# Strided attention and routed experts on one core: the values' products of two heads taken as one, with a block-diagonal second operand

## The chip, the cores and the metric

The kernel runs on one core of one Trainium2 chip. The metric is the device time of one execution in microseconds (us), measured on the chip. The engines are named as the profile names them: PE is TensorE's matmuls, PEld its weight loads, DVE is VectorE, ACT ScalarE, POOL GpSimd, SP SyncE, which here only issues transfers. All operands of the attention part are float32; a float32 matmul stands in the trace as two weight loads and two passes of the moving operand (the page counts each), a transpose as one of each.

## The reference

Attention over 8 batches, 8 heads, 576 positions, head dimension 64, and then a top-1 mixture of 8 experts on its rows. The first four heads see the last 32 positions, the other four see every 32nd position up to their own:

```
scores = scale * np.matmul(q, k.transpose(0, 1, 3, 2))
rel = pos[:, None] - pos[None, :]
mask_local = (rel >= 0) & (rel < stride)
mask_strided = (rel >= 0) & (pos[None, :] % stride == pos[:, None] % stride)
masks = np.stack([mask_local if h < H // 2 else mask_strided for h in range(H)], axis=0)
...
attn = np.matmul(attn / (sum + 1e-09), v)
x = attn.transpose(0, 2, 1, 3).reshape(B * S, H * D)
...
h = np.maximum(x[mask] @ w1[e], 0.0)
out[mask] = gate_w * eom * (h @ w2[e])
```

## The kernel before, in words

The attention part walks 40 steps, five for each batch (t = 5b + j). Rows of queries are cut into tiles: a strided tile has 64 rows (54 of them used: three residues of 18 rows) against 64 keys, a local tile 32 rows against 64 keys. Steps j = 0 and 1 hold only strided tiles, j = 3 and 4 only local tiles, j = 2 both. Each step holds two "windows" w of 128 rows, two pairs of heads i and in each pair two heads h. Head h = 0 of a pair lives on partitions 0 to 63 and head h = 1 on partitions 64 to 127, in queries (q_t), keys (kbs strided, kbl local) and values (vst strided, vlt and vev local: vlt as loaded, vev shifted by 32 positions by the copies of `even`).

A step is a chain over the engines that is worked off over five steps, so that PE always has several steps in hand. `scores` (L253) makes the products of queries and keys into sp, head by head: 64 rows of contraction, 64 or 32 rows of output. `bar` and `top` on DVE add the mask and take row maxima, `shift` on POOL subtracts them, `expo` on ACT takes the exponential. Two steps later `turn_p` transposes the probabilities on PE (four transposes of 128x128, in which the two heads of a pair come to lie on the two halves of the partitions) and `evac_p` copies them to SBUF as pt. Three steps later `values` (L304) multiplies pt with the values, and the column of ones behind each head's 64 values gives the sum of its row. Four steps later `norm` on DVE divides and writes x_t, `rows` sends x_t to DRAM (xd), `turn_x` transposes it and `evac_x` copies it, for the experts' logits (`logits`, L379) and the gating chain.

`values` takes each head by itself. Its loop is

```
for i, p0, m, n, h in packed(j, w):
    nc.tensor.matmul(out=xv[p0:p0 + m, h, w, i, :], lhsT=pt[half(h), w, i, p0:p0 + m],
                     rhs=value(b, i, h, m, n), start=True, stop=True)
```

where `half(h)` is the 64 partitions of a head: 64 rows of contraction, 64 (strided) or 32 (local) columns of weights, 65 moving columns. A strided step has 16 such matmuls, a local one 32, the mixed one 20. The two heads of a pair use the two row halves of the array, and the tiles at different p0 use different column groups. The outputs of head 0 and head 1 go to two banks of xp.

The order is written out by hand (`manual_schedule`): in each step PE runs scores of step t, turn_p of t - 2, values of t - 3, turn_x of t - 4, with pieces of the logits and the gating chain between them (`pump`). SP issues all loads of a batch: at j = 1 vst and at j = 3 vlt of the next batch (`load_v`, L209), one transfer over 128 partitions each; the two copies of vst and vlt alternate between batches. ACT issues no transfer in this part.

After the 40 steps a tail finishes the last batch, ranks the experts and starts the first expert's layer; then the experts' part (L751 to L791) runs matmuls over all 128 rows of the array to the end.

Of the kernel before, what the change touches and what calls it, by code (L numbers as in the profile page):

```python
# [7 lines left out]
F32 = mybir.dt.float32  # L8
# [9 lines left out]
B, H, S, D = 8, 8, 576, 64  # L18
# [12 lines left out]
NG = 11  # L31
# [26 lines left out]
def attn_moe_kernel(  # L58
# [109 lines left out]
    def attention():  # L168
        with ExitStack() as actx:
# [13 lines left out]
            kbl = [kv.tile([128, 2, 2, HS + 32], F32, name=f"kbl{i}") for i in range(2)]  # L183
            vlt = [kv.tile([128, NL, 2, D + 1], F32, name=f"vlt{i}") for i in range(2)]
            vst = [kv.tile([128, NG, 2, D + 1], F32, name=f"vst{i}") for i in range(2)]
            vev = kv.tile([128, NL, 2, D + 1], F32, name="vev")

            qts = {}

            def load_s(b, cs=slice(0, WS)):  # L190
# [18 lines left out]
            def load_v(b, ts, src):  # L209
                nc.sync.dma_start(out=ts[b % 2], in_=src[b])  # L210

            def even(b, eng, h, f):

                ps = slice(D * h + 32 * f, D * h + 32 * (f + 1))
                copy = nc.scalar.copy if eng is nc.scalar else eng.tensor_copy
                copy(out=vev[ps, f:NL].rearrange("p n i e -> p (n i e)"),
                     in_=vlt[b % 2][ps, 0:NL - f].rearrange("p n i e -> p (n i e)"))

# [10 lines left out]
            col0 = lambda g: 54 * g - 18 if g else 0  # L229

            half = lambda h: slice(D * h, D * (h + 1))

# [12 lines left out]

            def value(b, i, h, m, n):
                return (vst[b % 2] if m == 64 else vlt[b % 2] if n % 2 else vev)[half(h), n if m == 64 else n // 2, i, :]

# [55 lines left out]
            def values(b, j):  # L304
                pt = pt_.pop((b, j))
                xp = ps_x.tile([128, 2, 512], F32, name="xp")
                xv = xp[:, :, 0:260].rearrange("p h (w i e) -> p h w i e", w=2, i=2)
                for w in range(2):
                    for i, p0, m, n, h in packed(j, w):
                        nc.tensor.matmul(out=xv[p0:p0 + m, h, w, i, :], lhsT=pt[half(h), w, i, p0:p0 + m],  # L310
                                         rhs=value(b, i, h, m, n), start=True, stop=True)
                xp_[b, j] = xp[:, :, 0:260].rearrange("p h (g e) -> p h g e", g=4)

            def norm(b, j, part):
# [4 lines left out]
                if part == 0:  # L319
                    nc.vector.tensor_scalar(out=rs[:, 0], in0=xp[:, :, :, D], scalar1=1e-9, scalar2=None, op0=ALU.add)  # L320
                elif part == 1:
                    nc.vector.reciprocal(out=rs[:, 1], in_=rs[:, 0])
                else:
                    x_t = xp_p.tile([128, 2, 4, D], F32, name="x_t")
                    nc.vector.tensor_tensor(out=x_t.rearrange("p w (i h) d -> p h (w i) d", h=2), in0=xp[:, :, :, 0:D],
                                            in1=rs[:, 1].unsqueeze(3).to_broadcast([128, 2, 4, D]), op=ALU.mult)
                    x_[b, j] = x_t.rearrange("p w h d -> p w (h d)")
# [265 lines left out]
            nc.sync.dma_start(out=ident, in_=ident_in)  # L593
            for h in range(2):
                nc.vector.memset(vev[D * h + 32:D * (h + 1), 0], 0.0)
            load_v(0, vst, vs)
            load_v(0, vlt, vl)
            load_s(1)
            setup()

            ns = B * NS
            t = 0
            while t < ns:
# [29 lines left out]
                for h in ((0,) if b and j == 3 else (1,) if b and j == 4 else (0, 1) if t == 4 else ()):  # L633
                    even(b, nc.scalar, h, 1)
                    even(b, nc.vector, h, 0)
                at(expo, 0)
                if t + 1 < len(WARM):
                    warm(WARM[t + 1])
# [365 lines left out]
```

## Time and profile before

| | |
|---|---|
| time, three runs | 711.96, 713.33, 718.02 us; median 713.33 us |
| the profiled execution | 715.86 us; its span 714.2 us, so 1.66 us lie around the span |
| mean granted TensorE clock | 0.954 of full speed |
| busy in the span | PE 649.9 us (91%), PEld 541.1, DVE 306.0, ACT 260.8, POOL 187.3 |
| attention, 5 to 197 us | PE busy 149.3 us of 192 |
| experts, 260 us to the end | PE busy 446.5 us of 454 |

The busy time of PE counts passes whose ends are modelled and which overlap, so a PE that is busy all the time is not one at its peak: what counts is the distance between the starts of passes. "issue" as a releaser is time in which an engine stood still and waited for nothing that the profile shows. The granted clock of a stretch stands in the column PEclk of the table of stretches.

### The profile page before, as it was taken

The numbers are of one execution on the slowest core, as the hardware profiler recorded it, in microseconds if no ns is written. First come the engines' busy times: TensorE is split into PE (matmuls) and PEld (weight loads), VectorE is DVE, ScalarE is ACT, GpSimd is POOL, SyncE is SP. The second block draws the span as 40 slices with busy tenths as digits, with TensorE's granted clock in tenths as the row PEclk, the third lists the DMA queues.
The fourth block names the chain that finished last, engine by engine and source line by source line (L and its number), as shares of the span: only waits on it lengthen the run. The fifth ranks groups of instructions, "written<-read, shape, count | busy, mean of one in ns | idle before, by whom it ended". The sixth has DMA issues, their size and how long they took to land.

```text
span 714.2 us, 16814 instructions
## 1 busy us (share of the span) xinstructions
PE 649.9 (91%) x6965; PEld 541.1 (76%) x6965; DVE 306.0 (43%) x673; ACT 260.8 (37%) x483; POOL 187.3 (26%) x191
## 2 busy tenths in 40 slices
PE   6786877987777799999999999999999999999995
PEld 5564555655554588799879988988987987987984
DVE  3576657776544442433224232422633433432410
ACT  2464445445431431433323332423423423433420
POOL 3123354456342430140113013012201401301001
PEclk9799999897987899999999999999999999999998
DMA  8667556558524226352235133324524514521000
GB/s 313 258 213 251 156 194 225 168 170 271 160 67 146 56 73 216 118 182 60 90 104 154 40 134 121 117 58 144 153 75 133 160 31 140 163 96 58 15 14 38
DMA packets 42420, 95.26 MB, mean 133 GB/s; under 512 B 7219, under 2 KB 18067, under 8 KB 42344
## 3 DMA queue, kind: packets, MB, share of 16 engines
q1 hardware_dynamic: 33176, 71.24, 31.2%
q0 software_dynamic: 8048, 19.79, 8.5%
q10 hardware_dynamic: 1120, 3.15, 1.3%
q8 instruction: 55, 0.90, 0.5%
q14 instruction: 21, 0.17, 0.1%
HBM read 74.55 MB, written 20.47 MB: 133 GB/s over the span
## 4 chain that ended last, share of the span: by engine, by line
PE 61%; issue 23%; DMA 5%; POOL 4%; DVE 4%; SPq 1%; ACT 1%; another core or an unknown queue 1%; POOLq 0%; DVEq 0%; ACTq 0%
PE yp L774 22%; PE hp L758 20%; PE xp L310 4%; DMA xd<-x_t 4%; PE sp L258 4%; PE xtp L354 3%; PE tp L294 2%; PE sp L470 2%; POOL out_dram L791 2%; PE tp L748 2%; PE gp L386 1%; DMA kbl<-in_kl_dram 1%; POOL xg L153 1%; DVE p_t L270 1%; PE gp L395 1%
## 5 line engine op out<-in xcount | busy, mean ns | idle before, releaser
L758 PE MATMUL hp<-xh,w1l 128*128 128x256 f32 (+1 forms) x480 | 148.1, 309 | 0.0
L758 PE MATMUL hp<-xl,w1h 128*128 128x256 f32 (+1 forms) x480 | 148.0, 308 | 0.0
L758 PE MATMUL hp<-xh,w1h 128*128 128x256 f32 (+1 forms) x480 | 147.9, 308 | 0.0
L791 POOL DMA_INDIRECT out_dram<-ys,tab x40 | 41.9, 1047 | 352.1 <-ACT ys L790 340.9
L758 PEld LDWEIGHTS hp<-xh,w1h 128*128 128x128 f32 x480 | 91.2, 190 | 2.1
L758 PEld LDWEIGHTS hp<-xl,w1h 128*128 128x128 f32 x480 | 91.1, 190 | 1.9
L758 PEld LDWEIGHTS hp<-xh,w1l 128*128 128x128 f32 x480 | 91.0, 189 | 1.4
L774 PE MATMUL yp<-w2h,hhb 128*128 128x512 f32 (+3 forms) x208 | 83.9, 403 | 0.0
L774 PE MATMUL yp<-w2l,hhb 128*128 128x512 f32 (+3 forms) x208 | 82.2, 395 | 0.0
L774 PE MATMUL yp<-w2h,hlb 128*128 128x512 f32 (+3 forms) x208 | 81.7, 393 | 0.0
L696 DVE TENSOR_TENSOR xl<-tp,xh 128x512 fp32r<-128x512 f32 (+3 forms) x40 | 25.7, 650 | 114.4 <-ACT xh L695 114.4
L281 POOL TENSOR_TENSOR p_t<-p_t,st 128x512 f32<-128x512 f32 x40 | 47.2, 1179 | 104.0 <-DVE st L277 46.7
L762 DVE SCALAR_TENSOR_TENSOR hlb<-hp,hhb 128x480 fp32r<-128x480 f32 (+7 forms) x64 | 34.7, 541 | 84.9 <-ACT hhb L761 72.5
L761 ACT ACTIVATE hhb<-hp 128x480 fp32r<-128x480 f32 (+7 forms) x64 | 30.6, 478 | 100.7 <-PE hp L758 94.2
L695 ACT CAST xh<-tp 128x512 fp32r<-128x512 f32 (+3 forms) x40 | 21.8, 555 | 124.0 <-PE tp L748 124.0
L552 POOL DMA_INDIRECT table<-meta,dst x48 | 44.6, 929 | 30.7 <-DVE ew L497 13.3
L774 PE MATMUL yp<-w2h,hha 128*128 128x512 f32 x128 | 51.0, 398 | 0.0
L774 PE MATMUL yp<-w2h,hla 128*128 128x512 f32 x128 | 50.6, 395 | 0.0
L774 PE MATMUL yp<-w2l,hha 128*128 128x512 f32 x128 | 50.4, 394 | 0.0
L153 POOL DMA_INDIRECT xg<-xd,tab x40 | 44.8, 1119 | 17.8 <-issue 16.3
L287 ACT ACTIVATE p_t<-p_t 128x512 f32<-128x512 f32 x40 | 25.2, 630 | 61.1 <-POOL p_t L281 61.0
L762 DVE SCALAR_TENSOR_TENSOR hla<-hp,hha 128x256 fp32r<-128x256 f32 x56 | 23.6, 422 | 54.4 <-ACT hha L761 54.3
(134 smaller groups left out, 1068.5 us busy)
## 6 DMA issues: line engine op xcount, KB each, us to landing
raw<-in_moe_w_dram SPq DMA_DIRECT2D x54, 512.0 KB
vst<-in_vs_dram SPq DMA_DIRECT2D x8, 715.0 KB
kbl<-in_kl_dram SPq DMA_DIRECT2D x8, 640.0 KB
vlt<-in_vl_dram SPq DMA_DIRECT2D x8, 585.0 KB
q_t<-in_ql_dram SPq DMA_DIRECT2D x8, 576.0 KB
xd<-x_t SPq DMA_DIRECT2D x80, 54.0 KB
q_t<-in_qs_dram SPq DMA_DIRECT2D x7, 586.0 KB
kbs<-in_ks_dram SPq DMA_DIRECT2D x7, 586.0 KB
```

The lines of the kernel that those rows point to most:

```text
L153: nc.gpsimd.indirect_dma_start(out=dst, out_offset=None, in_=src, in_offset=bass.IndirectOffsetOnAxis(ap=idx, axis=0), bounds_check=top, o ...
L258: nc.tensor.matmul(out=sv[p0:p0 + m, h, w, i, :], lhsT=query(b, i, h, m, n), rhs=keys(b, i, h, m, n), start=True, stop=True)
L281: nc.gpsimd.tensor_tensor(out=p_[b, j], in0=p_[b, j], in1=sp_.pop((b, j)).unsqueeze(3).to_broadcast([128, 2, 4, 64]), op=ALU.subtract)
L287: nc.scalar.activation(out=p_t, in_=p_t, func=AF.Exp, scale=scale)
L310: nc.tensor.matmul(out=xv[p0:p0 + m, h, w, i, :], lhsT=pt[half(h), w, i, p0:p0 + m], rhs=value(b, i, h, m, n), start=True, stop=True)
L552: i = nc.gpsimd.indirect_dma_start(out=table[:, :], out_offset=bass.IndirectOffsetOnAxis(ap=dst[:, j:j + 1], axis=0), in_=meta[:, b * NB + ...
L696: nc.vector.tensor_tensor(out=lo, in0=src, in1=f32(hi), op=ALU.subtract)
L758: nc.tensor.matmul(out=hp[:, 0:n], lhsT=w[:, k, 128 * j:128 * (j + 1)], rhs=x[:, k, 0:n], start=first, stop=(k == KC - 1 and w is w1l))
L761: nc.scalar.activation(out=hh[:, j, 0:n], in_=hp[:, 0:n], func=AF.Relu)
L762: nc.vector.scalar_tensor_tensor(out=hl[:, j, 0:n], in0=hp[:, 0:n], scalar=0.0, in1=f32(hh[:, j, 0:n]), op0=ALU.max, op1=ALU.subtract)
L774: nc.tensor.matmul(out=yp[0:m, :], lhsT=h[:, j, o:o + m], rhs=w[:, j, :], start=(j == 0 and q == 0), stop=(j == FC - 1 and q == 2))
L791: i = nc.gpsimd.indirect_dma_start(out=out[:, :], out_offset=bass.IndirectOffsetOnAxis(ap=tab[:, 2:3], axis=0), in_=ys[0:m, :], in_offset= ...
```

## The change

The two heads of a pair are multiplied at once. The tiles of values get a new axis h in front (128, 2, n, 2, 65): partitions 0 to 63 hold head 0's values under h = 0 and zeros under h = 1, partitions 64 to 127 hold zeros under h = 0 and head 1's values under h = 1. One matmul then contracts over all 128 partitions of pt, and its 130 moving columns give both heads' 65 columns side by side. `scores` stays one head at a time. The layout of xp becomes one bank per window w instead of one per head, so `norm` writes x_t in plain order.

The zeros are written once per buffer by a new function `clear`: at the start for vlt[0] and vev on ACT (four copies of a zero column over 64 partitions x 1170 elements), for vst[0] on DVE and POOL (one memset each of 64 x 1430), and behind `expo` of steps 5 and 7 for vst[1] and vlt[1] on DVE and POOL. The loads write only the halves that hold values, so the zeros stay. `load_v` therefore needs two transfers in place of one: SP issues the half of head 0, ACT that of head 1, in the same places of the program. `even` copies the half of its head only.

```diff
-            vlt = [kv.tile([128, NL, 2, D + 1], F32, name=f"vlt{i}") for i in range(2)]
-            vst = [kv.tile([128, NG, 2, D + 1], F32, name=f"vst{i}") for i in range(2)]
-            vev = kv.tile([128, NL, 2, D + 1], F32, name="vev")
+            vlt = [kv.tile([128, 2, NL, 2, D + 1], F32, name=f"vlt{i}") for i in range(2)]
+            vst = [kv.tile([128, 2, NG, 2, D + 1], F32, name=f"vst{i}") for i in range(2)]
+            vev = kv.tile([128, 2, NL, 2, D + 1], F32, name="vev")
+
+            def clear(t, spare=False):
+                if spare:
+                    for ps, h in ((slice(0, D), 1), (slice(D, 128), 0)):
+                        o = t[ps, h].rearrange("p n i e -> p (n i e)")
+                        nc.scalar.copy(out=o, in_=zeros[ps, 0:1].to_broadcast([D, o.shape[1]]))
+                else:
+                    nc.vector.memset(t[0:D, 1], 0.0)
+                    nc.gpsimd.memset(t[D:128, 0], 0.0)
+                if t is vev:
+                    nc.vector.memset(t[32:D, 0, 0], 0.0)
+                    nc.gpsimd.memset(t[D + 32:128, 1, 0], 0.0)
...
             def load_v(b, ts, src):
-                nc.sync.dma_start(out=ts[b % 2], in_=src[b])
+                for h, eng in ((0, nc.sync), (1, nc.scalar)):
+                    eng.dma_start(out=ts[b % 2][half(h), h], in_=src[b, half(h)])
...
-            def value(b, i, h, m, n):
-                return (vst[b % 2] if m == 64 else vlt[b % 2] if n % 2 else vev)[half(h), n if m == 64 else n // 2, i, :]
+            def value(b, i, m, n):
+                return (vst[b % 2] if m == 64 else vlt[b % 2] if n % 2 else vev)[:, :, n if m == 64 else n // 2, i, :]
...
             def values(b, j):
                 pt = pt_.pop((b, j))
                 xp = ps_x.tile([128, 2, 512], F32, name="xp")
-                xv = xp[:, :, 0:260].rearrange("p h (w i e) -> p h w i e", w=2, i=2)
                 for w in range(2):
-                    for i, p0, m, n, h in packed(j, w):
-                        nc.tensor.matmul(out=xv[p0:p0 + m, h, w, i, :], lhsT=pt[half(h), w, i, p0:p0 + m],
-                                         rhs=value(b, i, h, m, n), start=True, stop=True)
-                xp_[b, j] = xp[:, :, 0:260].rearrange("p h (g e) -> p h g e", g=4)
+                    for i in range(2):
+                        for p0, m, n in tiles(j, w):
+                            nc.tensor.matmul(out=xp[p0:p0 + m, w, 130 * i:130 * (i + 1)],
+                                             lhsT=pt[:, w, i, p0:p0 + m], rhs=value(b, i, m, n), start=True, stop=True)
+                xp_[b, j] = xp[:, :, 0:260].rearrange("p w (h e) -> p w h e", h=4)
...
-                    nc.vector.tensor_tensor(out=x_t.rearrange("p w (i h) d -> p h (w i) d", h=2), in0=xp[:, :, :, 0:D],
+                    nc.vector.tensor_tensor(out=x_t, in0=xp[:, :, :, 0:D],
...
+            for v in (vlt[0], vev):
+                clear(v, spare=True)
+            clear(vst[0])
             load_v(0, vst, vs)
             load_v(0, vlt, vl)
...
+            clears = {5: vst[1], 7: vlt[1]}
...
                 at(expo, 0)
+                if t in clears:
+                    clear(clears[t])
```

What it does to the order of instructions, in three places. First PE, in steps 4 and 5, from the values of a strided step to the beginning of the values of the mixed one (xp is the product of values, xtp the transposed x_t, sp the scores, tp the transposed probabilities; behind each name the shape of output rows and moving columns). Before:

```order
L310 MATMUL xp<-vst_132,pt 64x65 x16
L354 MATMUL xtp<-ident,x_t 128x128 x4
L258 MATMUL sp<-kbs_127,q_t 64x64 x16
L294 MATMUL tp<-ident,p_t 128x128 x4
L310 MATMUL xp<-vst_132,pt 64x65 x8
L310 MATMUL xp<-vev,pt 32x65 x2
L310 MATMUL xp<-vlt_130,pt 32x65 x2
L310 MATMUL xp<-vst_132,pt 64x65 x2
```

and with the change:

```order
L322 MATMUL xp<-vst_132,pt 64x130 x8
L366 MATMUL xtp<-ident,x_t 128x128 x4
L270 MATMUL sp<-kbs_127,q_t 64x64 x16
L306 MATMUL tp<-ident,p_t 128x128 x4
L322 MATMUL xp<-vst_132,pt 64x130 x4
L322 MATMUL xp<-vev,pt 32x130
L322 MATMUL xp<-vlt_130,pt 32x130
L322 MATMUL xp<-vst_132,pt 64x130
```

Nothing changes its place; the products of values are half as many, with twice the columns, and everything else on PE is as it was.

Second ACT, in steps 7 and 8 of the program, around the load of vlt (xt takes the transposed x_t, pt the transposed probabilities, p_t is the exponential's tile). Before:

```order
L369 COPY xt<-xtp 128x6x18 x2
L372 COPY xt<-xtp 128x2x64
L373 COPY xt<-xtp 128x2x2x18
L301 COPY pt<-tp 128x512
L287 ACTIVATE p_t<-p_t 128x512
L363 COPY xt<-xtp 128x2x256
```

and with the change:

```order
L381 COPY xt<-xtp 128x6x18 x2
L384 COPY xt<-xtp 128x2x64
L385 COPY xt<-xtp 128x2x2x18
L313 COPY pt<-tp 128x512
L299 ACTIVATE p_t<-p_t 128x512
L224 DMA vlt_130<-in_vl_dram 64x1170
L375 COPY xt<-xtp 128x2x256
```

A transfer of 64 partitions now stands in ACT's queue between an exponential and the copy that frees xtp; the same happens at j = 1 with vst.

Third DVE, in steps 5 and 6, where a buffer of the second batch is cleared (rs holds the reciprocal row sums, st the maxima). Before:

```order
L270 TENSOR_TENSOR p_t<-sp,mask 128x2x4x64
L277 TENSOR_REDUCE st<-p_t 128x8
L320 TENSOR_SCALAR rs<-xp 128x8
L322 RECIPROCAL rs<-rs 128x8
L325 TENSOR_TENSOR x_t<-xp,rs 128x2x4x64
```

and with the change:

```order
L282 TENSOR_TENSOR p_t<-sp,mask 128x2x4x64
L289 TENSOR_REDUCE st<-p_t 128x8
L194 MEMSET vst_133 64x1430
L332 TENSOR_SCALAR rs<-xp 128x8
L334 RECIPROCAL rs<-rs 128x8
L337 TENSOR_TENSOR x_t<-xp,rs 128x512
```

A memset of 64 x 1430 has come in between the maxima of one step and the normalisation of the next, and x_t is written in one plain run.

More of the change, by code (lines that the diff above doesn't have):

```diff
@@ L183, in attention @@
             kbl = [kv.tile([128, 2, 2, HS + 32], F32, name=f"kbl{i}") for i in range(2)]
-            vlt = [kv.tile([128, NL, 2, D + 1], F32, name=f"vlt{i}") for i in range(2)]
-            vst = [kv.tile([128, NG, 2, D + 1], F32, name=f"vst{i}") for i in range(2)]
-            vev = kv.tile([128, NL, 2, D + 1], F32, name="vev")
+            vlt = [kv.tile([128, 2, NL, 2, D + 1], F32, name=f"vlt{i}") for i in range(2)]
[12 more added lines that the diff above has]
+                    nc.gpsimd.memset(t[D + 32:128, 1, 0], 0.0)
             qts = {}
+            half = lambda h: slice(D * h, D * (h + 1))
             def load_s(b, cs=slice(0, WS)):
@@ L215, in even @@
                 copy = nc.scalar.copy if eng is nc.scalar else eng.tensor_copy
-                copy(out=vev[ps, f:NL].rearrange("p n i e -> p (n i e)"),
-                     in_=vlt[b % 2][ps, 0:NL - f].rearrange("p n i e -> p (n i e)"))
+                copy(out=vev[ps, h, f:NL].rearrange("p n i e -> p (n i e)"),
+                     in_=vlt[b % 2][ps, h, 0:NL - f].rearrange("p n i e -> p (n i e)"))
             loc, srd = slice(0, 2), slice(2, 4)
@@ L229, in attention @@
             col0 = lambda g: 54 * g - 18 if g else 0
-            half = lambda h: slice(D * h, D * (h + 1))
             def query(b, i, h, m, n):
@@ L593, in attention @@
             nc.sync.dma_start(out=ident, in_=ident_in)
-            for h in range(2):
-                nc.vector.memset(vev[D * h + 32:D * (h + 1), 0], 0.0)
+            for v in (vlt[0], vev):
+                clear(v, spare=True)
+            clear(vst[0])
             load_v(0, vst, vs)
```

## The prediction

> **What bounds the kernel now.** I read the page's shares first, then the table of stretches, then who PE waited for, then the chain of waits in order of time.
>
> ```profile
> PE 649.9 (91%) x6965; PEld 541.1 (76%) x6965; DVE 306.0 (43%) x673; ACT 260.8 (37%) x483; POOL 187.3 (26%) x191
> q8 instruction: 55, 0.90, 0.5%
> ```
>
> Two numbers matter here. PE and PEld together execute 13930 instructions, and one queue carries 55 packets of 0.90/55 MB = 16 KB of instructions: one packet for 253 of PE's instructions. [...]
>
> ```profile
> 5.00:197.00 192.00, 149.28 (x4041) 110.00 (x4040) 125.17 (x336) 89.91 (x190) 78.22 (x74) 0.90 0.65 218
> 260.00:714.00 454.00, 446.45 (x2543) 391.38 (x2542) 150.14 (x237) 148.63 (x253) 84.53 (x85) 1.00 0.34 105
> ```
>
> The columns are the length, then busy time and count of PE, PEld, DVE, ACT and POOL, then granted clock, DMA share and GB/s. The experts' 454 us are bound by PE at full clock, and the change does not touch them. In the attention part PE is busy for 149 of 192 us and the clock is 0.90; no other engine is near its limit (DVE 125 of 192). So PE is the longest engine there, but 43 us of it are waits. The waits of PE in that stretch (us in total, times, longest):
>
> ```profile
> PE xp L310 <- issue: 14.6, 12, 4.3
> PE sp L258 <- issue: 8.7, 7, 2.4
> PE tp L294 <- issue: 4.2, 3, 2.7
> ...
> PE xtp L354 <- issue: 1.0, 1, 1.0
> ```
>
> 14.6 + 8.7 + 4.2 + 1.0 = 28.5 us in 23 waits are "issue": PE waits for no engine and no transfer of data. 4041 + 4040 instructions are 31.9 blocks of 253 in these 192 us, one per 6.0 us, 0.9 us of wait for each. I take these waits for the arrival of the next block of instructions. In the chain of waits (start, length, what) the long ones stand as
>
> ```profile
> 16.05 4.26 issue
> ...
> 25.04 1.70 issue
> ...
> 61.72 2.60 issue
> ...
> 69.67 1.96 issue
> ...
> 94.48 1.36 issue
> ```
>
> and behind each of these comes a stretch at half clock:
>
> ```profile
> 20.40:23.70 3.30, 3.30 (x104) 2.68 (x105) 2.66 (x6) 0.70 (x2) 0.05 (x1) 0.50 1.00 382
> 27.30:33.90 6.60, 6.60 (x116) 4.77 (x116) 3.58 (x7) 2.37 (x5) 1.04 (x1) 0.50 0.46 164
> ...
> 64.80:68.10 3.30, 3.30 (x85) 1.86 (x76) 0.85 (x3) 0.86 (x2) 1.24 (x2) 0.50 1.02 380
> 71.60:74.90 3.30, 3.27 (x41) 1.90 (x44) 1.06 (x3) 1.64 (x4) 1.84 (x2) 0.50 0.27 85
> 95.60:98.90 3.30, 3.06 (x41) 2.55 (x41) 0.35 (x1) 1.91 (x3) 2.83 (x3) 0.50 0.36 116
> 126.30:132.90 6.60, 6.60 (x140) 4.97 (x136) 4.20 (x17) 2.16 (x5) 3.14 (x4) 0.50 0.26 65
> 170.70:180.70 10.00, 9.42 (x182) 7.19 (x183) 4.29 (x11) 2.73 (x6) 4.68 (x5) 0.50 0.89 281
> ```
>
> PE is busy for 35.6 us in these seven stretches, so they cost about 17.8 us. The first five (19.5 us busy, 9.8 us lost) follow waits for instructions; the last two follow other waits. The attention part is thus PE's own work, plus waits for instructions, plus the slow clock that they leave behind.
>
> **The change part by part.** *The array's work.* What a pass costs is read from these rows of PE in order of time (start, length of the group, count), with the length of a single pass (min/median/max, ns) behind them:
>
> ```profile
> 42.33 0.69 PE L386 MATMUL gp<-xt,wgt 128*32 128x288 f32 x8
> 42.95 0.86 PE L258 MATMUL sp<-kbl,q_t 64*32 64x64 f32 x64
> ...
> 44.65 0.70 PE L310 MATMUL xp<-vst,pt 64*64 64x65 f32 x32
> ...
> 231.25 2.86 PE L470 MATMUL sp<-xe,raw 128*128 128x256 f32 x12 [0.78 <-DVE hla L477]
> ```
>
> ```profile
> L386 PE MATMUL gp<-xt,wgt x128: 403/430/690, 42.3 to 224.2; 128*32 128x288 f32 x128
> ```
>
> ```profile
> L310 PEld LDWEIGHTS xp<-vst,pt x704: 128/135/228, 15.4 to 203.8; 64*64 64x64 f32 x176
> L310 PE MATMUL xp<-vst,pt x704: 213/219/368, 15.4 to 203.9; 64*64 64x65 f32 x176
> ...
> L310 PE MATMUL xp<-vev,pt x576: 213/220/314, 28.8 to 217.2; 64*32 64x65 f32 x192
> ...
> L310 PE MATMUL xp<-vlt,pt x576: 213/237/314, 28.8 to 217.3; 64*32 64x65 f32 x192
> ```
>
> On the whole array 12 passes of 256 columns take 2.86 us; without the last one's 0.38 that is 11 distances of 0.225, or 0.88 ns per column. The eight passes of the logits (L386, all 128 rows, 32 columns of the array each) start within 0.69 - 0.43 = 0.26 us: two rounds of 288 columns x 0.88 = 0.25, so four tiles that lie side by side in the columns do run together. This row carries over to the new products, which also use all rows and 32 or 64 columns of the array.
>
> A round of 65 columns is 0.057 us, one of 130 is 0.114 us. Before, a strided step's 32 passes sit on 4 tiles of 64x64: 8 rounds, 0.46 us, and the row shows 0.70 - 0.22 = 0.48 us. Afterwards 16 passes sit on 2 tiles of 128x64: 8 rounds again, but of 130 columns: 0.91 us, so +0.46. A local step has 64 passes on 8 tiles of 64x32; there 64 passes start in 0.86 - 0.22 = 0.64 us (the scores' row, same shape), more than its 8 rounds of 0.057 = 0.46; afterwards 32 passes on 4 tiles are 8 rounds of 0.114 = 0.91 us: +0.27. The mixed step has 4 rounds of strided products, and four groups of two rounds for the others: 12 rounds, +0.68. A batch gains 2 x 0.46 + 0.68 + 2 x 0.27 = 2.14 us of PE, eight batches **+17.1 us**; a tenth of the stage is likely to stay at half clock, +1.7. Half of each block-diagonal operand is zeros, and the array streams them.
>
> [...]
>
> *Instructions.* The three groups of L310 are 704 + 576 + 576 = 1856 passes and as many loads. Half of both goes: 1856 instructions, 7.3 blocks. Within 5 to 197 us the last three steps' 168 passes are not contained; 1688 instructions and 6.7 blocks go, 25.2 remain. If each removed block took only its mean wait along, that is 6.7 x 0.9 = 6 us, the lower bound. The upper bound is all 28.5 us. [...] A block's other time is now (192 - 28.5)/31.9 = 5.1 us, and will be (163.5 + 18.8)/25.2 = 7.2 us. [...] The experts' stretch is the far end of this: 5085 instructions, 20 blocks, 23 us each, and no such wait. I take **-20 us**, nearer the upper bound.
>
> [...]
>
> *Clock.* [...] I take **-6 us**.
>
> *Clearing.* Prices from the rows of the start and of `even`:
>
> ```profile
> 0.87 1.28 ACT L287 ACT_TABLE_LOAD   x1 [0.87 <-PEq L994]
> 9.24 0.63 ACT L287 ACTIVATE p_t<-p_t 128x512 f32<-128x512 f32 x1 [7.08 <-POOL p_t L281]
> ...
> 23.58 2.13 ACT L216 COPY vev<-vlt 32x1040 f32<-32x1040 f32 x2
> ```
>
> ```profile
> 1.00 0.27 DVE L589 MEMSET xe<- 128x256 f32 x1 [1.00 <-PEq L994]
> ```
>
> ```profile
> 3.34 0.58 POOL L110 MEMSET xg<- 128x512 f32 x1
> ```
>
> Four copies of 1170 elements on ACT at 1.07 x 1170/1040 = 1.2 us are 4.8 us, behind the table load at 2.15: done at 7.0, two issues later at about 7.9, and the first exponential starts at 9.24 for POOL's sake. The cover is 1.3 us; without it the excess would delay the first step. DVE's and POOL's memsets of 1430 elements are about 0.27 x 1430/256 = 1.5 and 0.58 x 1430/512 = 1.6 us; at the start both engines are idle until the first scores. At steps 5 and 7 they stand in the way of the next normalisation and the next shift: 0 to 5.6 us together, since either is ready for a part of it; I take **+1 us**.
>
> *Transfers.* The same bytes, 16 issues more, on ACT.
>
> ```profile
> L210 SPq DMA_DIRECT2D vlt<-in_vl_dram x8: 354/438/1497, 6.5 to 169.7; - x8
> ```
>
> ACT, busy for 90 of 192 us, is held for 0.44 us in the usual case and 1.5 in the worst seen on SP; behind the issue stand the copies that free xtp and give pt, each needed by PE about half a step (2 us) later. Two of the 16 lie at the start; the other 14 cost between 0 and 14 x 1.5 = 21 us. The row's median lies well under that half step; I take **+1 us**. The wait that such a transfer carries is for products of a step already done.
>
> *Sum.* 17.1 + 1.7 - 20 - 6 + 1 + 1 = -5.2 us. The profiled execution took 715.86 us, 714.2 of span and 1.7 around it, so the change gives 710.7 on its basis; the median of the runs is 713.33, 2.5 us lower, and on that basis the forecast is **708 us**, 0.7% less than before. Its own range, with -25 to -14 for the waits and -8 to -4 for the clock, is 701 to 716.
>
> **The rivals.** *All waits for instructions and their slow clock go.* 17.1 + 1.7 - 28.5 - 9.8 + 2 = -17.5: 696 us. [...] Against it: the 4.26 us wait comes while the DMA is fullest, and blocks are fetched through the same DMA.
>
> *The waits do not get shorter, only fewer* (the other side). If a fetch starts late and each block costs its 0.9 us however long PE works on the last one, the gain is 6 us and the clock stays: 17.1 + 1.7 - 6 + 2 = +14.8: 728 us. It decides as soon as the term for instructions and clock together is under 21 us. For it: many waits come in steps of ordinary length; against it: the experts' 20 blocks without any.
>
> *Loads come into the open.* If in each round the next weights (128 ns at the least for 64 columns) are loaded only after it, 8 + 8 + 12 + 8 + 8 = 44 rounds per batch, 352 in all, get 0.10 to 0.13 us longer: about +40 on a forecast with all waits for instructions gone (-8.5): 740 us. Against it: the experts' stretch, and the logits' two rounds, whose second set of weights does not show.
>
> *ACT is held by its transfers.* 21 us in place of 1: 728 us. For it: SP's long issues when the DMA is full; against it: ACT's idle half.
>
> *The tiles do not run side by side with 64 columns each,* so that the products come one pass after another: 16 x 0.114 against 0.46 us in a strided step and more in a local one, about +9 us per batch: 780 us. The logits' row speaks against it.
>
> **How the numbers follow.** Forecast 0.48, all waits gone 0.24, waits only fewer 0.14, ACT held 0.06, loads in the open 0.04, no side by side 0.02, anything else 0.02. A measurement of this kernel tells about 1% from no change, that is 706.2 and 720.5 us. A third of the forecast's chance lies under 706.2, and nearly all of the first rival: 0.16 + 0.23 = 0.39 faster. Within 1%: 0.31 of the forecast and small parts of others, 0.36. Slower: 0.25, the other four and the forecast's upper tail. The range for 8 in 10 takes in the first rival and stops short of the two at 728: **694 to 725 us**.
>
> **What would show it.** In the changed profile the instruction queue has about 48 packets in place of 55; a strided step's values are 16 passes in about 1.1 us; PE's waits for "issue" in the attention part are under 12 us; fewer half-clock stretches stand before 100 us; ACT's copies still wait for PE, not PE for them. Values' groups much longer than 1.1 us, or waits for issue still at 20 us or more, would make the prediction wrong.

## The result, and the profile after

| | before | after |
|---|---|---|
| median of the runs on one chip (lowest to highest) | 715.6 us (711.96 to 718.02) | 737.37 us (731.31 to 739.5) |
| ratio, 95% interval | | 1.0295 [1.0209, 1.038] |
| profiled execution, span | 714.2 us | 737.5 us |

The change makes the kernel 2.95% slower, where 0.7% faster was forecast, and the time lies outside the range. What PE executes became less, as intended. The page of after, its engines and the two queues of SP (q1) and ACT (q10) with packets, MB and share of 16 engines:

```profile
PE 666.2 (90%) x6037; PEld 548.5 (74%) x6037; DVE 308.3 (42%) x675; ACT 267.1 (36%) x487; POOL 191.6 (26%) x195
q1 hardware_dynamic: 32152, 65.92, 29.7%
q10 hardware_dynamic: 2400, 8.47, 4.2%
q8 instruction: 48, 0.79, 0.5%
```

The same two queues on the page of before:

```profile
q1 hardware_dynamic: 33176, 71.24, 31.2%
q10 hardware_dynamic: 1120, 3.15, 1.3%
```

The bytes of both queues together are the same, 74.39 MB. The time that they take is not: (31.2 + 1.3)% of 714.2 us is 232 us of all 16 DMA engines before, (29.7 + 4.2)% of 737.5 us is 250 us after. The stretches of after, columns as in the prediction:

```profile
5.00:197.00 192.00, 147.71 (x2830) 104.65 (x2830) 111.92 (x296) 82.30 (x168) 71.42 (x68) 0.90 0.69 197
260.00:714.00 454.00, 452.42 (x2565) 396.07 (x2566) 163.76 (x252) 158.45 (x265) 86.27 (x87) 0.99 0.33 106
```

In the attention part every engine does less in the same 192 us than before (DVE 112 us of work against 125, ACT 82 against 90): the whole pipeline runs more slowly, while the DMA engines are busier (0.69 against 0.65) and move less (197 GB/s against 218). How far it falls back is read from the strided scores of all eight batches, whose last start ends the row (min/median/max of a pass, then first and last start in us). Before, then after:

```profile
L258 PE MATMUL sp<-kbs,q_t x704: 213/219/368, 5.5 to 182.8; 64*64 64x64 f32 x176
```

```profile
L270 PE MATMUL sp<-kbs,q_t x704: 213/218/367, 5.3 to 207.3; 64*64 64x64 f32 x176
```

The last of them starts 24.5 us later, at 207.3 us; the spans differ by 23.3 us. So the loss lies in the attention part. PE's waits of after between 5 and 197 us:

```profile
PE xp L322 <- DVE x_t L337: 15.6, 8, 2.9
PE sp L270 <- DMA kbs<-in_ks_dram: 12.5, 5, 5.1
PE sp L270 <- issue: 7.4, 12, 2.9
PE xp L322 <- issue: 3.7, 9, 0.8
...
PE tp L306 <- issue: 0.5, 2, 0.3
...
PE xp L322 <- POOL vlt L195: 0.5, 1, 0.5
```

The waits for issue are 11.8 us instead of 28.5 (a fourth line has 0.2), but two waits of the data's path stand at the head of the list: for the keys, and for the normalised x_t, which must be out of the way before xp's bank is free again. In before these two were small, even over 0 to 215 us:

```profile
PE sp L258 <- DMA kbs<-in_ks_dram: 3.7, 3, 2.8
PE xp L310 <- DVE x_t L325: 3.2, 2, 2.1
```

DVE's x_t in its turn waits for the write of an earlier x_t to memory; before and after (0 to 215 us):

```profile
DVE x_t L325 <- DMA xd<-x_t: 5.3, 4, 2.5
```

```profile
DVE x_t L337 <- DMA xd<-x_t: 21.2, 8, 4.0
```

Those writes go out on SP, and SP itself stood still for loads of values. The writes stand on two lines of the kernel, one for the local heads (L337 before, L349 after) and one for the strided heads (L342 before, L354 after). Before (0 to 215 us), only the writes of the local heads waited for strided values; after, both did, and the strided heads' writes for longer:

```profile
SPq L337 <- DMA vst<-in_vs_dram: 4.4, 5, 1.1
```

```profile
SPq L354 <- DMA vst<-in_vs_dram: 16.5, 6, 5.1
...
SPq L349 <- DMA vst<-in_vs_dram: 3.8, 5, 0.8
```

So the trace of after leads from PE over DVE to SP's line and to the value loads. That is a path; it does not yet say which of these waits costs the time. The change did four things at once: it cut each load into two transfers, put each half on 64 neighbouring partitions, gave one half to ACT's queue, and made the products of two heads one. The experiments take these apart.

### The profile page after: what moved, and what is told of

It reads as the page before. It is cut to its first block, busy times and chain, and to the rows that moved or that the text cites. A ratio compares the mean times of both kernels' runs of the same rounds, so it can differ in the third digit from the quotient of the medians.

```text
span 737.5 us, 15008 instructions
## 1 busy us (share of the span) xinstructions
PE 666.2 (90%) x6037; PEld 548.5 (74%) x6037; DVE 308.3 (42%) x675; ACT 267.1 (36%) x487; POOL 191.6 (26%) x195
## 3 DMA queue, kind: packets, MB, share of 16 engines
q1 hardware_dynamic: 32152, 65.92, 29.7%
## 4 chain that ended last, share of the span: by engine, by line
PE 53%; issue 19%; DMA 18%; POOL 3%; DVE 2%; SPq 1%; another core or an unknown queue 1%; ACT 0%; POOLq 0%; DVEq 0%; ACTq 0%
PE yp L791 21%; PE hp L775 19%; DMA kbs<-in_ks_dram 7%; DMA xd<-x_t 7%; DMA vst<-in_vs_dram 4%; PE xp L322 3%; PE sp L482 2%; PE sp L270 2%; POOL out_dram L808 2%; PE tp L765 2%; PE xtp L366 1%; POOL xg L153 1%; PE tp L306 1%; SPq L354 1%
## 5 line engine op out<-in xcount | busy, mean ns | idle before, releaser
L282 DVE TENSOR_TENSOR p_t<-sp,mask 128x512 f32<-128x512 f32 (+1 forms) x48 | 28.0, 598 | 61.3 <-PE sp L270 29.2
L564 POOL DMA_INDIRECT table<-meta,dst x48 | 44.5, 926 | 28.5 <-DVE ew L509 11.6
```

Of the source, the lines that this page charges most:

```text
L282: nc.vector.tensor_tensor(out=p_t[:, ws].rearrange("p w (i h) k -> p h (w i) k", h=2), in0=sv[:, :, ws].rearrange("p h w i k -> p h (w i) ...
L564: i = nc.gpsimd.indirect_dma_start(out=table[:, :], out_offset=bass.IndirectOffsetOnAxis(ap=dst[:, j:j + 1], axis=0), in_=meta[:, b * NB + ...
```

## The experiments

All ratios are to the kernel before, run on the same chip. Absolute times differ between chips (before: 695.2, 712.8, 713.7 and 693.8 us in the four groups below), so times are only compared within a group. The main theory is that the transfers cost the time and the products do not; its rivals are that the products cost it, or that ACT's queue does.

### First group: transfers or products

One queue for both halves; the rest is the change:

```
-                for h, eng in ((0, nc.sync), (1, nc.scalar)):
+                for h, eng in ((0, nc.sync), (1, nc.sync)):
```

> The changed kernel with both halves of each value load issued by SP; the block-diagonal products stay. Theory A (transfers): the 737 us of the change come from its split transfers, not from PE: the array's 16 us and the 13 us of saved waits for instructions nearly cancel. If it is ACT's queue that runs ahead of SP's keys and queries and takes their place, this kernel is back near 718 us, with PE's waits for kbs under 4 us; if it is the halves themselves (more transfers in the line of completion semaphores, 64 partitions each), it stays at 733 us or more. Rival B (array): the time goes into the products' longer passes and the queues do not matter: 737 us.

Measured: 712.05 us, ratio 1.0247 [1.0226, 1.0268]. Nearly all of the loss is still there without ACT's queue. A slower clock isn't its cause: the mean granted clock of whole executions was 0.966 in the four runs here and 0.968 in the runs of the kernel before on this chip.

The products of before, with only the loads cut as in the change:

```
-                nc.sync.dma_start(out=ts[b % 2], in_=src[b])
+                for ps, eng in ((slice(0, D), nc.sync), (slice(D, 128), nc.scalar)):
+                    eng.dma_start(out=ts[b % 2][ps], in_=src[b, ps])
```

> The kernel before, its products untouched, with only the value loads split into two halves of 64 partitions, SP's and ACT's. Theory A (transfers): most of the loss is here, 728 to 738 us, with DVE's waits for xd at 15 us or more and PE's waits for kbs near 12 us. Rival B (array): 714 to 718 us, as before.

Measured: 717.05 us, 1.0314 [1.028, 1.0347]: the whole loss, with none of the new products. (Here the granted clock was lower too, 0.951; what share of the loss came by way of it was not tried.) PE's waits (0 to 215 us) show the two of after:

```profile
PE sp L259 <- DMA kbs<-in_ks_dram: 23.2, 7, 4.9
PE xp L311 <- DVE x_t L326: 13.3, 7, 2.9
```

The other side, the products without most of the transfers. The value loads of batches 2, 3, 5, 6 and 7 are left out (their products use the values of an earlier batch), in the kernel before and in the changed one:

```
             def load_v(b, ts, src):
+                if b not in (0, 1, 4):
+                    return
```

> The kernel before with the value loads of batches 2, 3, 5, 6 and 7 left out; those batches are multiplied with the values that are still in the buffers. Reference for the next run: 705 to 714 us, a few us less than before since the traffic falls by 6.5 MB.

> The changed kernel with the value loads of batches 2, 3, 5, 6 and 7 left out in the same way; those batches are multiplied with the values that are still in the buffers. Theory A: without the transfers the two kernels come close, within 6 us of the run before it (the first steps' loads still differ, some 4 us). Rival B (array): 16 to 25 us above the run before it.

Measured: 676.89 us, 0.9791 [0.9718, 0.9864] with the products of before, 687.94 us, 0.9903 [0.9872, 0.9933] with the change. Both missed what was expected: the first gained more (705 to 714 us would have been 0.985 to 0.998 of before), and the second stayed 11 us above it where the main theory allowed 6. Two things follow all the same. The attention part is sensitive to its DMA: leaving out five of eight batches' values gains 2.1% although PE's work is the same. And the difference of the two falls from 2.95% to 1.1% (0.9903 - 0.9791), which is what three of eight loads would leave of it (3/8 x 2.95 = 1.1): as far as these intervals can tell, it goes with the loads, though the new products are all still there.

### Second group: place, number or bytes

The kernel before, again in two transfers on SP and ACT, but of every second partition each instead of 64 neighbours:

```
+                for h, eng in ((0, nc.sync), (1, nc.scalar)):
+                    eng.dma_start(out=ts[b % 2][h:128:2], in_=src[b, h:128:2])
```

> The kernel before, with its value loads split as in the run split only (SP and ACT, 64 partitions each, the same bytes and packets), but SP takes the even partitions and ACT the odd ones. Theory P (place): a transfer into 64 adjacent partitions moves at some 60% of the rate of one into 128, and that makes the keys and SP's line late; alternate partitions restore the rate: within 1% of before, q1 and q10 together need no larger share of the DMA than in the kernel before. Rival N (number): the two additional transfers per batch, each with a place in the line of completion semaphores, are the cause: 2% or more above before, as in split only.

Measured: 717.49 us, 1.0073 [1.004, 1.0105]. The same bytes, queues and number of transfers as above cost 0.7% instead of 3.1%. One part of the expectation failed: the two queues took 239 us of 16 engines (33.4% of 715.4), less than the 250 of the split into neighbours (34.9% of 715.3), but more than the 232 of before. The supposed rate of some 60% is near an estimate from the pages: the values' 10.65 MB (8 x 1300 KB) take 33 us at the 74.39 MB in 232 us of before, and with the 18 us that the neighbours add 51, which is 65%.

The change with the zeros loaded too: one transfer over 128 partitions on SP with the block-diagonal operand as it stands, double the bytes (the zeros are put into the input beforehand), and the same with the loads of batches 2, 3, 5, 6 and 7 left out:

```
-                for h, eng in ((0, nc.sync), (1, nc.scalar)):
-                    eng.dma_start(out=ts[b % 2][half(h), h], in_=src[b, half(h)])
+                nc.sync.dma_start(out=ts[b % 2], in_=src[b])
```

> The changed products with one transfer of all 128 partitions by SP per load, which brings the zeros from DRAM (double bytes, 10.4 MB more; only vev's zeros are still written on the chip). Theory P: the rate per byte is that of whole transfers, the bytes are double, so the DMA time is about that of the halves, and the loss is 1 to 2.5%. Rival N: as many transfers as before, so the loss falls to 0 to 1%. If the products themselves are the cause: 2 to 3%.

> The run with loaded zeros, with the value loads of batches 2, 3, 5, 6 and 7 left out as in the two runs with few loads; those batches use the values still in the buffers. Against the kernel before with few loads (0.979 of before) this shows the products nearly by themselves. If array (+16 us) and saved waits for instructions with their clock (-16 us) cancel: 0.975 to 0.985 of before. If the products lose by themselves: 0.99 to 1.00.

Measured: 734.7 us, 1.0306 [1.0248, 1.0363], and 705.9 us, 0.9883 [0.9824, 0.9942]. Twice the bytes over 128 partitions cost as much (1.0306) as the halves on 64 (1.0295). With few loads it is as fast (0.9883) as the changed kernel with few loads (0.9903). Neither came out as the theory had it: 3.06% is more than the 1 to 2.5% expected, and 0.9883 lies between the two ranges, nearer to the one for products that lose by themselves. Three eighths of 3.06% are again 1.1%, so what is left of the loads alone would put the second run at 0.99; this pair does not decide about the products, and the fourth group does.

The change with the two heads of a pair on alternate partitions, so that a half is every second partition. Keys are interleaved by the exponential, which writes k and h exchanged, and the products and the second operand stay block-diagonal, with their rows in another order (the transposes and `even` follow it); the buffers are cleared whole at the start by DVE and POOL:

```
-                    eng.dma_start(out=ts[b % 2][half(h), h], in_=src[b, half(h)])
+                    eng.dma_start(out=ts[b % 2][h:128:2, h], in_=src[b, half(h)])
...
-                nc.scalar.activation(out=p_t, in_=p_t, func=AF.Exp, scale=scale)
+                e_t = pp.tile([128, 4, 64, 2], F32, name="e_t")
+                nc.scalar.activation(out=e_t.rearrange("p g k h -> p g h k"), in_=p_t, func=AF.Exp, scale=scale)
```

> The changed kernel with the keys of two heads on alternate partitions: the exponential writes its result with the two heads interleaved, the loads of SP and ACT write even and odd partitions, all buffers are cleared whole at the start on DVE and POOL. Computes the same. Theory P: the transfers are as fast as before, so what is left is the products: 0.99 to 1.01 of before. Rival N: 1.02 to 1.03, as the change.

Measured: 717.82 us, 1.0051 [1.0016, 1.0087]. The place of the halves is worth 2.4% with the new products (1.0295 against 1.0051) and 2.4% with the old ones (1.0314 against 1.0073). The page of this kernel, the two queues:

```profile
q1 hardware_dynamic: 32152, 65.92, 28.8%
q10 hardware_dynamic: 2400, 8.47, 3.7%
```

With the span of 714.8 us that is 232 us of 16 engines, as before the change, where after took 250. On ACT's queue alone: 1120 of its packets are loads of the experts' weights, 1.3% x 714.2 x 16 = 149 us of one engine by the page of before. What is left for the 1280 packets of values is 4.2% x 737.5 x 16 - 149 = 347 us, 0.27 us each, in after, and 3.7% x 714.8 x 16 - 149 = 275 us, 0.21 us each, here. In the pair with the old products it is 0.29 us on neighbours and 0.24 on every second partition. PE's wait for x_t, 17.8 us in after, has nearly gone with it (0 to 215 us):

```profile
PE sp L258 <- DMA kbs<-in_ks_dram: 13.2, 7, 3.1
PE xp L312 <- issue: 5.1, 13, 0.6
PE xp L312 <- DVE x_t L327: 3.4, 3, 1.6
```

PE's wait for the keys has not gone, and SP's writes stand still for strided values for as long as ever:

```profile
SPq L344 <- DMA vst<-in_vs_dram: 23.1, 6, 4.7
```

So neither of these two is what the neighbours cost; of PE's waits it is the one for x_t that goes with them. Between 5 and 197 us PE waits 7.9 to 15.6 us for x_t in the four kernels that load all values on 64 neighbours (after, one queue, split only, and the first batch on SP below), and at most 5.6 us in the nine that load them all in another way.

### Third group: what is left

The alternate partitions with both halves on SP; the changed kernel with only the first batch's loads on SP; the alternate partitions with the loads of batches 2, 3, 5, 6 and 7 left out; and the kernel before with its alternate halves both on SP:

```
-                for h, eng in ((0, nc.sync), (1, nc.scalar)):
+                for h, eng in ((0, nc.sync), (1, nc.sync)):
...
-                for h, eng in ((0, nc.sync), (1, nc.scalar)):
+                for h, eng in ((0, nc.sync), (1, nc.scalar if b else nc.sync)):
```

> The change with the heads on alternate partitions, both halves of a load on SP's queue. With ACT's queue this kernel took 1.0051 of the kernel before. If the second queue is what remains of the loss (ACT's first half of the strided values goes out ahead of SP's second keys, and the second step's scores begin at about 12.5 us against 8.3 before), the second step begins near 8.5 us and the ratio is 0.995 to 1.000. If the number of transfers is what remains (16 more in SP's line of transfers, each of which waits for the one eight back), SP's line gets later and the ratio is 1.005 to 1.012.

> The changed kernel, with the first batch's four half loads on SP, all others as the change has them. If the loss comes from the place of the halves (64 adjacent partitions), in all eight batches, it stays: a ratio of 1.02 to 1.03, at most 4 us less than the changed kernel, by the second step's scores back from 12.5 to about 8.5 us. If the disturbed start were the source of what follows, the ratio falls to 1.005 or less.

> The change with the heads on alternate partitions, with the value loads of batches 2, 3, 5, 6 and 7 left out (their products use the values already there). The kernel before with the same loads left out took 0.979 of the kernel before, the changed kernel with them left out 0.990. If the products of two heads by themselves are worth nothing (array time against waits for instructions), 0.977 to 0.983. If they cost what those two differ by (1.1%), 0.988 to 0.992, and the place of the halves would not be the whole loss. If they gain and the transfers hid it, under 0.975.

> The kernel before with each value load as two transfers of alternate partitions, both on SP. With ACT's queue for the second it took 1.0073 of the kernel before. If the queue of ACT is what costs those 0.7%, 0.998 to 1.003; if the number of transfers does, 1.006 to 1.012. Beside the run with the change's products on the same two transfers of SP it also gives what the products do by themselves: equal within 0.3% if array and waits cancel.

Measured: 708.01 us, 0.9895 [0.9802, 0.9989]; 732.08 us, 1.0251 [1.0153, 1.0349]; 703.39 us, 0.9827 [0.9719, 0.9934]; 713.07 us, 0.9972 [0.9919, 1.0025]. The changed kernel keeps its loss with the start put right, and the second queue costs 1.0% with the old products (1.0073 against 0.9972) and 1.6% with the new ones (1.0051 against 0.9895). The run with few loads lies nearer to the kernel before with few loads (0.9791) than to the change (0.9903), but its interval excludes neither. The first number, below both ranges that were given for it, looked like a version faster than before, but its interval nearly reaches 1, and its clock in the attention part had been good, 0.97 of full speed against 0.84 for the kernel before with the same transfers, so both were run again with more rounds.

### Fourth group: the products by themselves, and where the second queue costs

> The change with the heads on alternate partitions and all loads on SP, a second time with more rounds, beside the kernel before with the same transfers. Measured first: 0.9895 of the kernel before, with an interval that reaches from 0.980 to 0.999. If the products by themselves gain what the prediction's sum gave (5 us), 0.988 to 0.994 here and 0.7% under the kernel before with the same transfers; if array and waits only cancel, 0.997 to 1.003 and no difference to it.

> The kernel before with each value load as two transfers of alternate partitions on SP, a second time with more rounds. If 16 transfers more cost nothing on one queue, 0.996 to 1.003; if they cost half of what two queues did, 1.004.

> The change with the heads on alternate partitions, the first batch's halves on SP, those of the other batches on SP and ACT. On two queues throughout it took 1.0051, on SP alone 0.9895. If ACT's queue costs only at the start (its first half ahead of SP's keys), this equals the run on SP alone. If it costs in every batch (in the trace with two queues SP's line waits 23 us for strided values against under 4 us with one), it stays within 0.3% of 1.005.

The third is the alternate layout with the second edit above: the first batch on SP, the others on both queues. Measured: 695.86 us, 1.0019 [1.0001, 1.0036]; 696.25 us, 1.0027 [1.0004, 1.0049]; 702.19 us, 1.0123 [1.0087, 1.016]. The gain of the first run on SP alone was not confirmed. With equal transfers the new products and the old differ by 0.4 us in 696, less than can be told apart. (Two more things differ between these kernels, the clearing at the start and the exponential that interleaves, 671 ns each against 630.) The third run missed its range: 1.0123 is more than 1.005, the ratio with both queues throughout, which was measured on another chip. Within this group the second queue costs 1.0% (702.19 against 695.86) though the start is on SP: so it costs in the batches and not only at the start.

What it does there is seen in SP's waits (0 to 215 us), first with everything on SP, where it is the local heads' writes that wait, then with both queues, where it is the strided heads' (L344):

```profile
SPq L339 <- DMA vst<-in_vs_dram: 3.1, 9, 0.5
```

```profile
SPq L344 <- DMA vst<-in_vs_dram: 23.2, 6, 5.8
```

The keys are issued by SP too, and PE waits longer for them (5 to 197 us), again with everything on SP and then with both queues:

```profile
PE sp L258 <- DMA kbs<-in_ks_dram: 14.8, 5, 3.9
```

```profile
PE sp L258 <- DMA kbs<-in_ks_dram: 19.7, 6, 4.5
```

The other two pairs on alternate partitions agree, 8.0 and 13.2 us with the new products, 4.6 and 13.3 with the old. In the pair on neighbours the wait for x_t grows instead (7.9 to 15.6).

One of the six waits of a write (L344) for a load of values, between 46 and 61 us of the kernel with both queues, and the issues around it (start, length of the issue):

```profile
SPq L344 <- DMA vst<-in_vs_dram: 3.5, 1, 3.5
```

```profile
47.80 11.53 SPq L344 DMA_DIRECT2D xd<-x_t  x8
52.05 0.49 ACTq L212 DMA_DIRECT2D vst<-in_vs_dram  x1
59.43 0.53 SPq L212 DMA_DIRECT2D vst<-in_vs_dram  x1
```

SP issues its own half of vst only at 59.43, behind the group of eight writes. The load for which a write in that group stood 3.5 us is thus ACT's, issued at 52.05. A write of x_t uses none of its data. What it waits for is a count. The trace of after, whose loads of the later batches stand in the same places of the program, keeps for each transfer the completion count (a semaphore) that it raises and the one that it waits for: before 215 us the 186 transfers of SP and ACT go round among eight counts as in one line, and each of the 178 behind the first eight waits for the count that it will raise, which the transfer eight places ahead raised last. ACT's load of vst issued at 58.67 has its place in that line ahead of the eight writes of the group that starts at 54.78. It raises its count for the last time at 65.58, and the sixth write, eight places behind it, goes out at 65.60; in the batch before it is 39.10 and 39.11. With everything on SP the strided values stand behind those eight writes, and the local writes that come eight places later hardly wait (0.5 us at most, 3.1 in all). So it is shown that the load on ACT makes SP wait, and by which count; that these waits are all of the 1.0% was not tried by itself.

## Why the prediction was wrong

The step that failed is *Transfers*: "The same bytes, 16 issues more, on ACT", taken at +1 us. It priced a transfer by its bytes and by the time in which ACT is held, and never asked where a half lands, nor who else waits for it. In its place the runs show two costs: the place of the halves, 2.3 to 2.4% (1.0247 against 1.0019 on one queue, 1.0295 against 1.0051 on two), about 17 us; and the second queue, 1.0% in the pair of one group (1.0123 against 1.0019), about 7 us. Three other pairs give 0.5% for the queue (1.0295 against 1.0247, less than their intervals can tell), 1.0% (1.0073 against 0.9972) and 1.6% (1.0051 against 0.9895, the number that was not confirmed). Together these are about 24 us, where the change lost 22 (737.37 against 715.6). The error of 29 us (737 against 708) is the 22 us, the 5 us that were forecast for the products and that the pair with most runs doesn't show, and 2 us by which the kernel before ran longer beside the change (715.6) than in the runs that the forecast stands on (713.33).

That neighbours cost more shows in the times, 1.0314 against 1.0073 on every second partition with the old products on two queues, and in the packets of values on ACT's queue, 0.29 us against 0.24 with the old products and 0.27 against 0.21 with the new ones. Why a packet takes longer on neighbours no run here shows.

Point by point:

- *The array's work*, +17.1 us: right. A strided step's 16 passes take 1.11 us in after, where 32 took 0.70: +0.41 for a predicted +0.46. The row (start, length of the group):

```profile
20.17 1.11 PE L322 MATMUL xp<-vst,pt 128*64 128x130 f32 x16
```

  and a single pass in it (min/median/max, ns):

```profile
L322 PE MATMUL xp<-vst,pt x352: 271/273/480, 20.2 to 229.4; 128*64 128x130 f32 x176
```

  From the first pass of values to the first instruction behind them, at full clock, it is 0.42 us more in a strided step (1.05 against 0.63), 0.62 in the mixed one (2.03 against 1.41), 0.24 in a local one (1.03 against 0.79): (2 x 0.42 + 0.62 + 2 x 0.24) x 8 = 15.5 us. Loads in the open and tiles that don't run side by side, the two rivals on the array, are out.

- *Instructions*, -20 us: 48 packets as forecast, and 28.5 us of waits for issue became 11.8. But that isn't what was gained. The 28.5 us are one execution's: four other profiles with the same old products (their loads split) have 12.4 to 15.6 us, so the base of the term did not hold for other executions. With equal transfers (both on SP, alternate partitions) the old products had these, and 0.5 us for L295 beside them:

```profile
PE xp L311 <- issue: 7.6, 5, 2.5
PE sp L259 <- issue: 4.3, 3, 2.0
```

  and the new ones this:

```profile
PE sp L258 <- issue: 3.1, 1, 3.1
```

  That is 9.3 us less, half the term. The other two pairs with equal transfers give 4.8 us (12.7 and 7.9, two queues) and 4.1 (15.6 and 11.5, one queue), under the lower bound of 6. So the term has the right sign and was two to five times too large. No trace names what a wait for issue waits for, and how it depends on the time between two blocks, from which the size was taken, no run shows; what the runs show in its place are these 4.1 to 9.3 us.

- *Clock*, -6 us: 0.90 in the changed kernel as before, so nothing in the change as it stands. From which length on a wait leaves a slow clock behind, on which the term stood, no run shows: in before, PE's waits of 1.75 us at 46.76 and 1.53 at 57.24 lie in a stretch at full clock,

```profile
46.76 1.75 issue
...
57.24 1.53 issue
```

```profile
34.10:64.60 30.50, 23.57 (x781) 17.76 (x770) 22.59 (x61) 17.27 (x38) 10.05 (x9) 1.00 0.64 214
```

  while the shorter one of 1.70 at 25.04 has a stretch at 0.50 behind it. With equal transfers the new products had 0.92 and the old 0.88:

```profile
5.00:197.00 192.00, 157.17 (x3216) 113.66 (x3215) 127.12 (x344) 93.10 (x195) 84.57 (x83) 0.92 0.66 218
```

```profile
5.00:197.00 192.00, 153.07 (x4086) 113.77 (x4085) 128.52 (x344) 93.16 (x195) 82.14 (x78) 0.88 0.65 220
```

  0.04 of 192 us is 7.7. This isn't the chance of one execution: the mean granted clock of whole executions was 0.974 against 0.965 in these two kernels (12 runs each), and 0.968 against 0.948 and 0.975 against 0.951 in the other two pairs. As (1 - clock) x span that is 6.5, 13.8 and 16.6 us. So the term has the right sign, and its size changes from pair to pair. Array +15.5, waits for issue -9.3 and clock -6.5 come to -0.3 us, where -0.4 was measured; the other pairs come to -3.1 (measured +0.3) and -5.2 (measured -5.1, not confirmed). This is an estimate, as the waits are those of single executions. The products cancel, or gain little, where the prediction had -5.2 with the same signs.

- *Clearing*, +1 us: as taken or less. PE waited once, 0.5 us, for POOL's clearing of vlt (the row stands above). The start is another matter. ACT, which waited for nothing there, sent its half of the values at 2.18 us, ahead of SP's second keys:

```profile
2.18 0.56 ACTq L224 DMA_DIRECT2D vst<-in_vs_dram  x1
3.54 0.61 SPq L207 DMA_DIRECT2D kbs<-in_ks_dram  x1
12.46 0.82 PE L270 MATMUL sp<-kbs,q_t 64*64 64x64 f32 x20 [5.08 <-DMA kbs<-in_ks_dram]
```

  Before, the second scores started at 8.32 us. The 4 us at the start are real, but the kernel with the first batch on SP, whose second scores start at 8.84, still took 1.0251: they are a small part.

- Of the rivals, "Loads come into the open", 740 us, came nearest in time, and by luck: the 16 passes in 1.11 us show no such load. "The waits do not get shorter, only fewer", 728 us, had 6 us for the waits, which lies in the measured 4 to 9, and a clock that stays, which holds for the change as it stands and not with equal transfers. "ACT is held by its transfers", also 728 us, is wrong in its mechanism. ACT's issues are short:

```profile
L224 ACTq DMA_DIRECT2D vst<-in_vs_dram x8: 472/473/562, 2.2 to 171.6; - x8
```

  The price was on the transfer's way and on SP's line, not on ACT. The sentence "The wait that such a transfer carries is for products of a step already done" looked at what the transfer waits for, and not at who will wait for the transfer.

- The signs named ahead came true: the packets, the length of the values, the waits for issue (11.8 against "under 12"), four half-clock stretches before 100 us in place of five, and ACT's copies, for which PE waits 0.5 us in all. The two signs that were to prove the prediction wrong stayed away. They did not decide, as all of them speak of PE and ACT; none of them watched the DMA's share or SP's waits.

## What to carry to other kernels

A load that is cut in two is not the same load (1.0314 on 64 neighbours here, 1.0073 on every second partition): ask which partitions each piece covers, compare the time of the queues at equal bytes, and if the operand must be split by heads, interleave the heads over the partitions instead of giving each 64 neighbours. A transfer that is moved to another engine's queue can still keep its place in the line of completion counts, as ACT's load did eight places ahead of the write that stood for it until 65.60 us of after; look which later transfer waits for its count. And a wait that one trace shows is not a price (28.5 us for issue in one, 12.4 to 15.6 in four others): look at more executions, and measure with equal transfers and both kinds of products before pricing it in full.

## What the runs showed of the hardware that was not expected

- Loads of 64 neighbouring partitions took 0.27 us per packet on ACT's queue, of every second partition 0.21, at the same bytes. On one queue, for the same 33432 packets and 71.25 MB, the change with neighbours (first row, span 712.7 us) used 239 us of 16 engines, with alternate partitions (second, span 695.1, another chip) 220; on a third chip the latter used 220 too (31.1% of 706.0):

```profile
q1 hardware_dynamic: 33432, 71.25, 33.6%
```

```profile
q1 hardware_dynamic: 33432, 71.25, 31.7%
```

- The attention part pays for traffic that no wait of PE for data names: without five of eight value loads the kernel before took 0.9791 [0.9718, 0.9864] of its time. PE's waits for keys and x_t were not shorter in its profile (13.7 us against 6.9). Its waits for issue were (12.7 us against 28.5, one execution each, not of one group), and its granted clock was higher (0.979 against 0.968, means of the runs on one chip). Why was not tried.
- With 128 rows and 64 columns of the array, the 16 passes of 130 moving columns started within 0.84 us (1.11 less the last one's own 0.27), the 32 passes of 65 before, whose two heads ran side by side, within 0.48. So joining the heads cost array time and saved none. A weight load of 64 columns (132 ns at the least in after) did not stand in the open between the passes, which started 0.056 us apart in the mean.
